# Attention and a residual MLP in one kernel: beta's rows on GpSimd, a later a1 and token mix, and the third batch's late q

## The chip, the cores and the metric

The kernel runs on one core of a Trainium2 chip. The time is the device time of one launch in microseconds (us), the median of several runs. A profile is one further execution, taken by the hardware profiler; its span is a little shorter than the device time. Five engines work side by side: TensorE (PE, matmuls; its weight loads are listed as PEld), VectorE (DVE), ScalarE (ACT), GpSimd (POOL) and SyncE (SP, which here only issues transfers). "L410" is line 410 of the kernel.

## The reference, cut to what matters

Eight batches of 384 tokens. Grouped attention (16 query heads, 4 key heads, head size 64) gives x of width 1024, and x goes through a residual MLP with a mix over tokens and one over channels:

```python
scores = scale * np.matmul(q, k.transpose(0, 1, 3, 2))
attn = np.exp(scores - max) / (sum + 1e-09)
x = np.matmul(attn, v)                       # (B, 384, 1024)

a1 = alpha1 * x + beta1
tok = np.einsum('ts,bsd->btd', w_tok, a1)    # mix over the 384 tokens
u = x + lam * tok
a2 = alpha2 * u + beta2
ch = np.maximum(a2 @ w_ch1, 0.0) @ w_ch2     # 1024 -> 4096 -> 1024
out = u + lam * ch
```

All inputs are float32 in DRAM; the kernel casts to bfloat16 while loading or afterwards.

## The kernel before

One batch's MLP is "main(b)": 32 tiles of h (w_ch1 times a2, ReLU), then six tiles of ch (w_ch2 times hT). The attention, token mix and transposes of batch b + 1 are "side(b + 1)", small pieces of work that are put between the matmuls of main(b) at numbered steps. w_ch1 is streamed again for each batch through a ring of five chunks; w_ch2 is loaded once, during the first batch. The first batch's own attention, side(0), has nothing to hide behind: it runs alone at the start.

Loads and transposes of k and q (k2 holds k twice, side by side; "flip" is a DMA transpose into kT or qT):

```python
def load_q(b):
    qrs[b] = sb.tile([P, Hq, NST, D], bf, tag="q_raw", name="q_raw", bufs=1)
    for h in range(0, Hq, G):
        nc.gpsimd.dma_start(out=qrs[b][:, h:h + G], in_=q[b, h:h + G]...)

def flip_queue(b):
    return nc.scalar if b == 2 else nc.sync

def flip_q(b, i=0, n=NP):
    flip_queue(b).dma_start_transpose(out=qT[:, i:i + n]..., in_=qrs[b][:, 2 * i:2 * (i + n)]...)
```

In the first batch (`first`), the normalization of one pair of heads, a1 and the token mix:

```python
def av_piece(p, hh):
    ...                                              # 18 matmuls for the pair p
    nc.vector.reciprocal(out=rinv, in_=av[:, :, :, D:])
    nc.vector.tensor_tensor(out=x[:, :, cols(p)]..., in0=av[...], in1=rinv..., op=MUL)
    if first:
        a1s[p] = hTf[...]                            # three places in turn
        nc.vector.tensor_tensor(out=a1s[p], in0=x[:, :, cols(p)], in1=bc(g1, p), op=MUL)
        return
    ...

def tok(p):
    ps = bank([P, NST, P], "mm", "tok") if first else ...
    for tt in range(NST):
        for st in range(NST):
            nc.tensor.matmul(out=ps[:, tt, :], lhsT=wtokT[...], rhs=a1s[p][:, st, :], ...)
        if first:
            nc.tensor.matmul(out=ps[:, tt, :], lhsT=R[...], rhs=H[:, cols(p)], ...)  # beta's part
    nc.vector.tensor_tensor(out=u, in0=ps, in1=u, op=ADD)
```

Scores go to PSUM banks "sc", of which there are two in side(0), and exp on ScalarE empties them. The order of side(0): 18 steps, each begins with scores(i), and behind it come the listed pieces. `ut` is the transpose of u (a2_transpose), `h_part` the first matmuls of main(0), `wtok_transpose` turns w_tok, `scale_rows` and `split` prepare alpha1 (row 0), beta1 (row 1) and alpha2, beta2 (rows 2, 3) in two bfloat16 parts, `spread` copies such a row to all partitions with a matmul, `rows_r` and `fill_h` build R and H for beta's part of the token mix:

```python
at = {0: [(warmup, 3), (scale_rows, 0), (split, 0, 1, 0)], 1: [(k_transpose, 1, 1), (split, 0, 1, 1)],
      2: [(q_transpose, 2, 2, "av")], 3: [(warmup, 1), (spread, lower, (0, 1), "tp")],
      4: [(av, 0)], 5: [(wtok_transpose, 0, "av"), (wtok_transpose, 1, "tp")],
      6: [(av, 1), (wtok_transpose, 2, "av"), (k_transpose, 2, 2, "tp")], 7: [(q_transpose, 4, 2, "av"), (scale_rows, 1), (split, 1, 2)],
      8: [(fill_h, 0), (rows_r, "tp"), (av, 2)], 9: [(spread, upper, (0, 1), "av", "ACT"), (q_transpose, 6, 2, "mm")],
      10: [(tok, 0)],
      11: [(av, 3)], 12: [(tok, 1), (ut, 0)], 13: [(av, 4), (tok, 2)], 14: [(ut, 1), (fill_h, 4), (tok, 3)],
      15: [(av, 5), (ut, 2)], 16: [(tok, 4), (ut, 3)], 17: [(av, 6), (tok, 5)]}
```

The weight ring in main(b), the load of the third batch (index 2), and where its flips stand in main(1) (steps 46 to 62 of the 64 half-tiles of h):

```python
            if b or c + RING < NCH:
                load_w1(b * NCH + c + RING)
            ...
            if b == 0 and c == NCH - 1:
                for i in range(RING):
                    load_w1(NCH + i)
                load_next(2)              # place_k twice, load_q, load_v
...
            if b == 1:
                moves = [(0, 46 + 4 * i, flip_q, 2, 2 * i - 2, 2) if i else (0, 46, flip_k, 2) for i in range(5)]
```

The issues of GpSimd at the start:

```python
load_v(0)
nc.gpsimd.dma_start(out=wtok_in, ...)
load_q4(2)
load_q4(3)
place_k(0, 0, (0,))
for c in range(RING):
    load_w1(c)
place_k(0, 1)            # casts k on GpSimd
```

Of the kernel before, what the change touches and what calls it, by code (L numbers as in the profile page):

```python
# [12 lines left out]
def kernel(  # L13
# [21 lines left out]
    nc = tc.nc  # L35
# [3 lines left out]
    RELU = mybir.ActivationFunctionType.Relu  # L39
    MUL = mybir.AluOpType.mult  # L40
    ADD = mybir.AluOpType.add

    B, Hq, S, D = q.shape
    Hkv = k.shape[1]
# [3 lines left out]
    P = 128  # L48
    NST = S // P
# [3 lines left out]
    NP = Hq // 2  # L53
# [3 lines left out]
    RING = 5  # L57
# [56 lines left out]
        for h in range(0, Hq, G):  # L114
            nc.gpsimd.dma_start(out=qrs[b][:, h:h + G], in_=q[b, h:h + G].rearrange("h (p st) d -> p h st d", st=NST))

    def flip_queue(b):
        return nc.scalar if b == 2 else nc.sync

    def flip_k(b):  # L120
        flip_queue(b).dma_start_transpose(out=kT.rearrange("p st h s -> p (st h) s"),
                                    in_=k2s[b].rearrange("p st h a d -> p (st h a d)"))

    def flip_q(b, i=0, n=NP):
        flip_queue(b).dma_start_transpose(out=qT[:, i:i + n].rearrange("p a j s -> p (a j) s"),
                                    in_=qrs[b][:, 2 * i:2 * (i + n)].rearrange("p h st d -> p (h st d)"))

    w1src = moe_w_ch1.rearrange("(dt di) nf -> di dt nf", di=P)
# [45 lines left out]
    def side(b):  # L174
# [8 lines left out]
        def cols(p):  # L183
            return slice(p * P, (p + 1) * P)
# [54 lines left out]
        def av_piece(p, hh):  # L239
            if hh == 0:  # L240
                if first:
                    avs[p] = bank([P, 2, NST, D1], "mm", "av")
                else:
                    avs[p] = three()[:, 0].rearrange("p k s -> p (k s)")[:, :2 * NST * D1].rearrange(
                        "p (h st d) -> p h st d", h=2, st=NST)
            av = avs[p]
            hk = (2 * p + hh) // G
            for sq in range(NST):
                m = NST * hh + sq
                for sk in range(NST):  # L250
                    k = (p * NST + sk) * NST + m // 2
                    nc.tensor.matmul(out=av[:, hh, sq, :], lhsT=ess[k // 4][:, m % 2, k % 4, :],  # L252
                                     rhs=vb[:, sk, hk, :], start=(sk == 0), stop=(sk == NST - 1))
            if hh == 0:
                return
            rinv = sb.tile([P, 2, NST, 1], f32, tag="rinv", name="rinv", bufs=1)
            nc.vector.reciprocal(out=rinv, in_=av[:, :, :, D:])  # L257
            nc.vector.tensor_tensor(out=x[:, :, cols(p)].rearrange("p st (h d) -> p h st d", h=2), in0=av[:, :, :, :D],  # L258
                                    in1=rinv.to_broadcast([P, 2, NST, D]), op=MUL)
            if first:  # L260
                a1s[p] = hTf[:, 6144 + p % 3 * S:6144 + (p % 3 + 1) * S].rearrange("p (a d) -> p a d", a=NST)
                nc.vector.tensor_tensor(out=a1s[p], in0=x[:, :, cols(p)], in1=bc(g1, p), op=MUL)
                return
            t = sb.tile([P, NST, P], f32, tag="tmp", name="a1f", bufs=4)
            nc.vector.tensor_tensor(out=t, in0=x[:, :, cols(p)], in1=bc(g1, p), op=MUL)  # L265
            a1s[p] = sb.tile([P, NST, P], bf, tag="a1", name="a1", bufs=2)
            nc.vector.tensor_tensor(out=a1s[p], in0=t, in1=bc(h1, p), op=ADD)  # L267

        def tok(p):
            ps = bank([P, NST, P], "mm", "tok") if first else three()[:, 0, :NST]  # L270
# [79 lines left out]
        if not first:  # L350

            turns = {}
            if b == 1:
# [19 lines left out]
        ut = a2_transpose  # L373
        at = {0: [(warmup, 3), (scale_rows, 0), (split, 0, 1, 0)], 1: [(k_transpose, 1, 1), (split, 0, 1, 1)],
              2: [(q_transpose, 2, 2, "av")], 3: [(warmup, 1), (spread, lower, (0, 1), "tp")],
              4: [(av, 0)], 5: [(wtok_transpose, 0, "av"), (wtok_transpose, 1, "tp")],
              6: [(av, 1), (wtok_transpose, 2, "av"), (k_transpose, 2, 2, "tp")], 7: [(q_transpose, 4, 2, "av"), (scale_rows, 1), (split, 1, 2)],
              8: [(fill_h, 0), (rows_r, "tp"), (av, 2)], 9: [(spread, upper, (0, 1), "av", "ACT"), (q_transpose, 6, 2, "mm")],
              10: [(tok, 0)],
              11: [(av, 3)], 12: [(tok, 1), (ut, 0)], 13: [(av, 4), (tok, 2)], 14: [(ut, 1), (fill_h, 4), (tok, 3)],  # L380
              15: [(av, 5), (ut, 2)], 16: [(tok, 4), (ut, 3)], 17: [(av, 6), (tok, 5)]}
        for i in range(18):
            add(scores, i)
            for f, *a in at.get(i, []):
                add(f, *a)
        for f, *a in ((ut, 4), (h_part, (0, 1), range(4)), (av, 7), (ut, 5), (tok, 6),
                      (h_part, (2, 3), range(4)), (h_part, range(4), (4,)), (ut, 6), (tok, 7),
                      (h_part, range(4), (5,)), (ut, 7), (h_part, range(4), (6,)), (h_part, range(4), (7,))):
            add(f, *a)
        return us  # L390
# [8 lines left out]
    def main(b):  # L399
# [3 lines left out]
        for c in range(NCH):  # L403
            w1 = w1_tiles.pop(b * NCH + c)
            for j in range(CW):
                nt = c * CW + j
                begun = b == 0 and nt in early
                ps = early[nt] if begun else bank([P, 512], "mm", "h")
                for dt in range(0 if begun else NDT):
                    nc.tensor.matmul(out=ps[:, :n], lhsT=w1[:, dt, j * P:(j + 1) * P],  # L410
                                     rhs=a2T[:, dt, :n], start=(dt == 0), stop=(dt == NDT - 1))
                    if dt == 3:
                        yield 0
                c1 = bias1[:, nt:nt + 1]
                if b == 0:
                    evac("DVE" if nt % 2 else "ACT")(out=c1, in_=ps[:, S:n])
                if nt % 2 == 0:
                    nc.scalar.activation(out=hT[:, nt, :], in_=ps[:, :S], func=RELU, bias=c1)  # L418
                else:
                    nc.vector.tensor_scalar(out=hT[:, nt, :], in0=ps[:, :S], scalar1=c1,  # L420
                                            scalar2=0.0, op0=ADD, op1=mybir.AluOpType.max)
                yield 0

            if b or c + RING < NCH:
                load_w1(b * NCH + c + RING)
            if b == 0 and c == NCH - RING:
                for i in range(3, 8):
                    load_w2(0, i, 8)
                for i in range(8):
                    load_w2(1, i, 8)  # L430
            if b == 0 and c == NCH - 1:
                for i in range(RING):
                    load_w1(NCH + i)
                load_next(2)
        for dw in range(NDW):
            cs = slice(dw * 512, (dw + 1) * 512)
            for ms in range(NST):
# [17 lines left out]
    with tc.manual_schedule(engines=order):  # L455
# [59 lines left out]
                nc.vector.tensor_reduce(out=t[:n], in_=ident[:n, :n].rearrange("p (k c) -> p c k", c=NP), op=ADD, axis=AX)  # L515


        def scale_rows(i):
            r = rows_f[:, i * P:(i + 1) * P]
            nc.vector.tensor_tensor(out=r, in0=r, in1=rows_f[:, 3 * P:4 * P], op=MUL)  # L520


        def split(lo, hi, step=None):
            c = slice(lo * P, hi * P)
            for i, m in enumerate(masks[:2]):
                if step in (None, i):
                    src, dst = (rows_t, rows_f) if i else (rows_f, rows_t)
                    nc.vector.tensor_copy(out=rows_b[:32, c], in_=src[:, c])
                    nc.vector.scalar_tensor_tensor(out=dst[:, c], in0=rows_b[:32, c], scalar=m, in1=src[:, c],
                                                   op0=MUL, op1=mybir.AluOpType.subtract)  # L530
            if step != 0:
                nc.vector.tensor_copy(out=rows_b[:32, c], in_=rows_f[:, c])


        def fill_h(p):
# [2 lines left out]
                                    in1=sel4[:, p:p + 4, None].to_broadcast([32, 4, P]), op=MUL)  # L538

        load_v(0)  # L540
        nc.gpsimd.dma_start(out=wtok_in, in_=moe_w_tok.rearrange("(p tt) s -> p tt s", tt=NST))
        load_q4(2)
        load_q4(3)
        place_k(0, 0, (0,))
        for c in range(RING):
            load_w1(c)
        place_k(0, 1)

        load_k(1)
        load_q(1)  # L550
# [8 lines left out]
        for b in range(B):  # L559
            us = side(b + 1) if b + 1 < B else ({}, {})  # L560


            moves = []
            if b == 1:
                moves = [(0, 46 + 4 * i, flip_q, 2, 2 * i - 2, 2) if i else (0, 46, flip_k, 2) for i in range(5)]
            if 0 < b < B - 2:
                moves += [(1, 1, load_k, b + 2), (1, 2, load_next, b + 2), (1, 34, flip_k, b + 2), (1, 36, flip_q, b + 2, 0, 2),
                          (1, 37, flip_q, b + 2, 2, 2), (1, 42, flip_q, b + 2, 4, 2), (1, 43, flip_q, b + 2, 6, 2)]
            for i, u, *m in moves:
                us[i].setdefault(u, []).append(m)  # L570
            done = [0, 0]
            for second in main(b):
                if b == second - done[1] - 1 == 0:
                    lead_banks.close()
                    threes.append(ST(tc.psum_pool(name="threes", bufs=3)))
                for f, *a in us[second].get(done[second], []):
                    f(*a)
                done[second] += 1
# [28 lines left out]
```

The softmax here doesn't subtract the row's maximum and nothing guards it: scores larger than these inputs give would overflow.

## Time and profile before

| | |
|---|---|
| time, median of 3 runs | 806.16 us (805.33 to 807.13) |
| span of the profiled run | 803.5 us, granted TensorE clock 1.000 |
| TensorE busy | 793.8 us, 6123 matmuls |
| w_ch chunks loaded | 144 of 512 KB (as written), issued by GpSimd, median 8.6 us to landing |
| DMA traffic | 113.17 MB, mean 141 GB/s |
| first batch's side(0) | ends at 38.48 us, when main(0)'s own h begins |
| second batch's h | begins at 133.44 us |
| third batch's h | begins at 232.67 us |

An entry of the timeline gives the start, the duration, the engine, the line, the operation, the tiles, how many instructions were merged, and in brackets how long the engine had stood idle before and who released it. Matmul ends are modelled, so small holes between matmuls can be hidden in a "busy" TensorE; differences of starts are safer than durations.

### The profile page before, as it was taken

The page shows a single profiled execution, that of the slowest core. Times are in us where ns is not written, and L with a number is a line of the kernel's source. Part 1 is how long each engine was busy: PE and PEld are TensorE (multiplying, and loading weights), DVE is VectorE, ACT ScalarE, POOL GpSimd, SP SyncE. Part 2 cuts the span into 40 slices and gives each one's busy share as a digit, 9 for nine tenths or more (in the row PEclk, how much of TensorE's full clock was granted, in tenths as well). Part 3 has the DMA queues.
Part 4 walks back from the last instruction along what each step waited for, and adds up shares of the span by engine and source line. Part 5 has one row for each costly group of instructions (what it writes and reads, how often), then busy time and mean ns, then how long its engine had stood idle before and what let it go on. Part 6 is the DMA issues. An engine that isn't in the chain of part 4 may idle for free.

```text
span 803.5 us, 14220 instructions
## 1 busy us (share of the span) xinstructions
PE 793.8 (99%) x6123; PEld 452.0 (56%) x6123; DVE 343.5 (43%) x669; ACT 226.9 (28%) x309; POOL 178.5 (22%) x233
## 2 busy tenths in 40 slices
PE   8999999999999999999999999999999999999997
PEld 4766555655556555565555655566555655556545
DVE  8652465215552266322662236622366225552122
ACT  6624431223402233123221233122431223312100
POOL 7234231332013500135002340033400330003000
PEclk9999999999999999999999999999999999999999
DMA  9999999999269972999439991499914995129611
GB/s 190 202 186 202 205 207 170 187 186 170 66 126 188 198 101 58 162 189 196 74 73 169 193 196 43 92 174 197 163 46 114 165 198 88 48 61 187 82 40 40
DMA packets 234975, 113.17 MB, mean 141 GB/s; under 512 B 84376, under 2 KB 228768, under 8 KB 234912
## 3 DMA queue, kind: packets, MB, share of 16 engines
q0 software_dynamic: 170752, 83.47, 79.1%
q1 hardware_dynamic: 58848, 27.22, 13.5%
q10 hardware_dynamic: 5312, 1.57, 1.5%
q8 instruction: 48, 0.79, 0.4%
q14 instruction: 15, 0.12, 0.0%
HBM read 170.53 MB, written 12.58 MB: 228 GB/s over the span
## 4 chain that ended last, share of the span: by engine, by line
PE 84%; DMA 10%; issue 3%; DVE 1%; POOL 1%; ACT 0%; POOLq 0%
PE ch L443 37%; PE h L410 34%; DMA w<-in_moe_w_ch_dram 8%; PE sc L217 4%; PE sc L252 3%; PE sc L273 3%; DMA qT<-q_raw 1%; POOL w L136 1%; PE h L168 1%; PE tok L273 1%; PE av L252 0%; PE warm L460 0%; PE ut L290 0%; PE tp L203 0%; ACT hT L226 0%
## 5 line engine op out<-in xcount | busy, mean ns | idle before, releaser
L443 PE MATMUL ch<-w,hT 128*128 128x512 bf16 (+2 forms) x1600 | 357.7, 371 | 1.1 <-DVE o L448 0.9
L410 PE MATMUL h<-a2T,w 128*128 128x384 bf16 (+1 forms) x2016 | 331.5, 326 | 0.8 <-ACT hT L418 0.8
L410 PEld LDWEIGHTS <-w 128*128 128x128 bf16 x2016 | 196.8, 98 | 131.2 <-issue 1.5
L443 PEld LDWEIGHTS <-hT 128*128 128x128 bf16 x1600 | 144.6, 98 | 153.1 <-issue 10.5
L136 POOL DMA_DIRECT2D w<-in_moe_w_ch_dram x128 | 112.1, 878 | 519.3 <-PE h L410 500.5
L226 ACT ACTIVATE es<-sc 128x1024 bf16<-128x1024 f32 x126 | 121.4, 1023 | 187.9 <-PE sc L217 175.8
L420 DVE TENSOR_SCALAR hT<-h,bias 128x384 bf16<-128x384 f32 x128 | 79.1, 618 | 218.3 <-PE h L410 217.7
L418 ACT ACTIVATE hT<-h,bias 128x384 bf16<-128x384 f32 x128 | 74.3, 580 | 304.9 <-PE h L410 299.4
L448 DVE TENSOR_TENSOR o<-ch,vecs 128x512 f32<-128x512 f32 (+2 forms) x50 | 33.4, 669 | 107.8 <-PE ch L443 107.8
L252 PEld LDWEIGHTS <-es 128*128 128x128 bf16 x1008 | 38.2, 97 | 13.2
L273 PEld LDWEIGHTS <-wtokT 128*128 128x128 bf16 x576 | 37.3, 98 | 13.8 <-DVE x L258 1.7
L217 PE MATMUL sc<-qT,kT 64*128 64x384 bf16 (+2 forms) x576 | 41.9, 272 | 0.7 <-DMA qT<-q_raw 0.6
L257 DVE RECIPROCAL rinv<-sc 128x6 f32<-128x6 f32 x56 | 10.8, 193 | 68.4 <-PE sc L252 67.5
L252 PE MATMUL sc<-v,es 128*128 128x65 bf16 x1008 | 39.9, 193 | 0.0
L280 DVE TENSOR_TENSOR x<-sc,x 128x384 f32<-128x384 f32 x56 | 31.0, 553 | 20.0 <-PE sc L273 20.0
L273 PE MATMUL sc<-a,wtokT 128*128 128x128 bf16 x504 | 37.3, 219 | 0.0
L217 PEld LDWEIGHTS <-kT 64*128 64x128 bf16 x576 | 21.6, 94 | 24.5 <-issue 18.2
L449 DVE TENSOR_TENSOR o<-o,x 128x512 f32<-128x512 f32 (+2 forms) x50 | 33.5, 670 | 1.7
L284 DVE TENSOR_TENSOR a<-x,vecs 128x384 bf16<-128x384 f32 x56 | 32.7, 584 | 1.9
L265 DVE TENSOR_TENSOR a1f<-x,vecs 128x384 f32<-128x384 f32 x56 | 31.2, 558 | 1.9
L267 DVE TENSOR_TENSOR a<-a1f,vecs 128x384 bf16<-128x384 f32 x56 | 31.2, 558 | 1.9
L258 DVE TENSOR_TENSOR x<-sc,rinv 128x384 f32<-128x384 f32 x56 | 31.2, 558 | 1.9
(75 smaller groups left out, 203.1 us busy)
## 6 DMA issues: line engine op xcount, KB each, us to landing
w<-in_moe_w_ch_dram POOLq DMA_DIRECT2D x144, 512.0 KB, 8.6
out_dram<-o SPq DMA_DIRECT2D x47, 256.0 KB, 2.0
q_raw<-in_q_dram POOLq DMA_DIRECT2D x28, 192.0 KB, 8.1
kst<-in_k_dram SPq DMA_DIRECT2D x16, 192.0 KB, 3.4
v<-in_v_dram POOLq DMA_DIRECT2D x24, 64.0 KB, 7.9
a2T<-a SPq DMA_TRANSPOSE x56, 2.3
qg<-in_q_dram POOLq DMA_DIRECT2D x3, 192.0 KB, 5.9
stage<-in_q_dram ACTq DMA_DIRECT2D x2, 192.0 KB, 3.7
```

Source lines behind the costliest of these rows:

```text
L136: nc.gpsimd.dma_start(out=t, in_=w1src[:, :, c * CW * P:(c + 1) * CW * P])
L217: nc.tensor.matmul(out=sc[:, hh, k % 4:k % 4 + n], lhsT=kT[r, sk, 2 * p // G, :], rhs=qT[r, p, st:st + n, :], start=True, stop=True)
L226: nc.scalar.activation(out=e, in_=sc, func=EXP, scale=scale_qk)
L252: nc.tensor.matmul(out=av[:, hh, sq, :], lhsT=ess[k // 4][:, m % 2, k % 4, :], rhs=vb[:, sk, hk, :], start=(sk == 0), stop=(sk == NST - 1))
L273: nc.tensor.matmul(out=ps[:, tt, :], lhsT=wtokT[:, st, tt * P:(tt + 1) * P], rhs=a1s[p][:, st, :], start=(st == 0), stop=(st == NST - 1 an ...
L284: nc.vector.tensor_tensor(out=a2s[p], in0=u, in1=bc(al2, p), op=MUL)
L410: nc.tensor.matmul(out=ps[:, :n], lhsT=w1[:, dt, j * P:(j + 1) * P], rhs=a2T[:, dt, :n], start=(dt == 0), stop=(dt == NDT - 1))
L418: nc.scalar.activation(out=hT[:, nt, :], in_=ps[:, :S], func=RELU, bias=c1)
L420: nc.vector.tensor_scalar(out=hT[:, nt, :], in0=ps[:, :S], scalar1=c1, scalar2=0.0, op0=ADD, op1=mybir.AluOpType.max)
L443: nc.tensor.matmul(out=ps[:, lo:hi], lhsT=hT[:, nt, ms * P:(ms + 1) * P], rhs=w2[:, nt, dw * 512 + lo:dw * 512 + hi], start=(nt == 0), sto ...
L448: nc.vector.tensor_tensor(out=o[:, lo:hi], in0=ps[:, lo:hi], in1=lam_t[:, c], op=MUL)
L449: nc.vector.tensor_tensor(out=o[:, lo:hi], in0=o[:, lo:hi], in1=x[:, ms, c], op=ADD)
```

## The change

For the third batch: q is loaded later, behind the last w_ch1 chunk of the second batch, so that it does not stand in the stream before; the flips of k and q go to SP's queue; k is turned at the second batch's first step, q in four parts as they land. For the first batch: beta1's row is scaled and split on GpSimd, early; k's cast on GpSimd comes before most weight chunks; q's third group is loaded before w_tok; w_tok's transposes come later; a1 is a piece of its own, apart from AV; the token mix begins three steps later; the upper half of alpha1's spread is emptied by VectorE and not by ScalarE.

```diff
-    def flip_queue(b):
-        return nc.scalar if b == 2 else nc.sync
     def flip_q(b, i=0, n=NP):
-        flip_queue(b).dma_start_transpose(...)
+        nc.sync.dma_start_transpose(...)            # flip_k likewise
...
             if first:
-                a1s[p] = hTf[...]
-                nc.vector.tensor_tensor(out=a1s[p], in0=x[:, :, cols(p)], in1=bc(g1, p), op=MUL)
                 return
+        def a1(p):
+            a1s[p] = hTf[...]
+            nc.vector.tensor_tensor(out=a1s[p], in0=x[:, :, cols(p)], in1=bc(g1, p), op=MUL)
...
-              4: [(av, 0)], 5: [(wtok_transpose, 0, "av"), (wtok_transpose, 1, "tp")],
-              6: [(av, 1), (wtok_transpose, 2, "av"), (k_transpose, 2, 2, "tp")], 7: [(q_transpose, 4, 2, "av"), (scale_rows, 1), (split, 1, 2)],
-              8: [(fill_h, 0), (rows_r, "tp"), (av, 2)], 9: [(spread, upper, (0, 1), "av", "ACT"), (q_transpose, 6, 2, "mm")],
-              10: [(tok, 0)],
-              11: [(av, 3)], 12: [(tok, 1), (ut, 0)], 13: [(av, 4), (tok, 2)], 14: [(ut, 1), (fill_h, 4), (tok, 3)],
-              15: [(av, 5), (ut, 2)], 16: [(tok, 4), (ut, 3)], 17: [(av, 6), (tok, 5)]}
+              4: [(av, 0)], 5: [(a1, 0)], 6: [(av, 1), (k_transpose, 2, 2, "tp")],
+              7: [(q_transpose, 4, 2, "av"), (a1, 1)], 8: [(av, 2)],
+              9: [(wtok_transpose, 0, "av"), (wtok_transpose, 1, "tp")],
+              10: [(wtok_transpose, 2, "av"), (q_transpose, 6, 2, "mm"), (fill_h, 0)], 11: [(av, 3), (rows_r, "tp")],
+              12: [(spread, upper, (0, 1), "av"), (a1, 2)], 13: [(tok, 0), (av, 4), (a1, 3)],
+              14: [(tok, 1), (ut, 0), (a1, 4)], 15: [(av, 5), (tok, 2), (a1, 5), (fill_h, 4)], 16: [(ut, 1), (tok, 3)],
+              17: [(ut, 2), (av, 6), (a1, 6)]}
...
-        for f, *a in ((ut, 4), (h_part, (0, 1), range(4)), (av, 7), (ut, 5), (tok, 6),
-                      (h_part, (2, 3), range(4)), (h_part, range(4), (4,)), (ut, 6), (tok, 7),
+        for f, *a in ((tok, 4), (ut, 3), (h_part, (0, 1), range(3)), (av, 7), (a1, 7), (tok, 5), (ut, 4), (h_part, (0, 1), (3,)),
+                      (tok, 6), (h_part, (2, 3), range(4)), (ut, 5), (tok, 7), (h_part, range(4), (4,)), (ut, 6),
                       (h_part, range(4), (5,)), (ut, 7), (h_part, range(4), (6,)), (h_part, range(4), (7,))):
...
             if b == 0 and c == NCH - 1:
                 for i in range(RING):
                     load_w1(NCH + i)
-                load_next(2)
+                place_k(2, 0)
+                place_k(2, 1)
+                load_v(2)
+            if b == 1 and c == NCH - RING - 1:
+                load_q(2)
...
+        def split(lo, hi, step=None, eng=nc.vector):
+            ...                                   # on GpSimd: tensor_scalar, then tensor_tensor,
+            ...                                   # for VectorE's one scalar_tensor_tensor
...
         load_v(0)
+        load_q4(2)
         nc.gpsimd.dma_start(out=wtok_in, ...)
-        load_q4(2)
         load_q4(3)
         place_k(0, 0, (0,))
-        for c in range(RING):
+        load_w1(0)
+        load_w1(1)
+        place_k(0, 1)
+        scale_rows(1, nc.gpsimd)
+        split(1, 2, None, nc.gpsimd)
+        for c in range(2, RING):
             load_w1(c)
-        place_k(0, 1)
...
             if b == 1:
-                moves = [(0, 46 + 4 * i, flip_q, 2, 2 * i - 2, 2) if i else (0, 46, flip_k, 2) for i in range(5)]
+                moves = [(0, 1, flip_k, 2)] + [(0, 46, flip_q, 2, i, 2) for i in range(0, NP, 2)]
```

More of the change, by code (lines that the diff above doesn't have):

```diff
@@ L41 @@
     ADD = mybir.AluOpType.add
+    SUB = mybir.AluOpType.subtract
     B, Hq, S, D = q.shape
@@ L115, in load_q @@
             nc.gpsimd.dma_start(out=qrs[b][:, h:h + G], in_=q[b, h:h + G].rearrange("h (p st) d -> p h st d", st=NST))
-    def flip_queue(b):
-        return nc.scalar if b == 2 else nc.sync
     def flip_k(b):
-        flip_queue(b).dma_start_transpose(out=kT.rearrange("p st h s -> p (st h) s"),
+        nc.sync.dma_start_transpose(out=kT.rearrange("p st h s -> p (st h) s"),
                                     in_=k2s[b].rearrange("p st h a d -> p (st h a d)"))
     def flip_q(b, i=0, n=NP):
-        flip_queue(b).dma_start_transpose(out=qT[:, i:i + n].rearrange("p a j s -> p (a j) s"),
+        nc.sync.dma_start_transpose(out=qT[:, i:i + n].rearrange("p a j s -> p (a j) s"),
                                     in_=qrs[b][:, 2 * i:2 * (i + n)].rearrange("p h st d -> p (h st d)"))
@@ L260, in av_piece @@
             if first:
-                a1s[p] = hTf[:, 6144 + p % 3 * S:6144 + (p % 3 + 1) * S].rearrange("p (a d) -> p a d", a=NST)
-                nc.vector.tensor_tensor(out=a1s[p], in0=x[:, :, cols(p)], in1=bc(g1, p), op=MUL)
                 return
@@ L267, in av_piece @@
             nc.vector.tensor_tensor(out=a1s[p], in0=t, in1=bc(h1, p), op=ADD)
+        def a1(p):
+            a1s[p] = hTf[:, 6144 + p % 3 * S:6144 + (p % 3 + 1) * S].rearrange("p (a d) -> p a d", a=NST)
+            nc.vector.tensor_tensor(out=a1s[p], in0=x[:, :, cols(p)], in1=bc(g1, p), op=MUL)
         def tok(p):
@@ L515, with scale_rows @@
                 nc.vector.tensor_reduce(out=t[:n], in_=ident[:n, :n].rearrange("p (k c) -> p c k", c=NP), op=ADD, axis=AX)
-        def scale_rows(i):
+        def scale_rows(i, eng=nc.vector):
             r = rows_f[:, i * P:(i + 1) * P]
-            nc.vector.tensor_tensor(out=r, in0=r, in1=rows_f[:, 3 * P:4 * P], op=MUL)
-        def split(lo, hi, step=None):
+            eng.tensor_tensor(out=r, in0=r, in1=rows_f[:, 3 * P:4 * P], op=MUL)
+        def split(lo, hi, step=None, eng=nc.vector):
             c = slice(lo * P, hi * P)
@@ L527, in split @@
                     src, dst = (rows_t, rows_f) if i else (rows_f, rows_t)
-                    nc.vector.tensor_copy(out=rows_b[:32, c], in_=src[:, c])
-                    nc.vector.scalar_tensor_tensor(out=dst[:, c], in0=rows_b[:32, c], scalar=m, in1=src[:, c],
-                                                   op0=MUL, op1=mybir.AluOpType.subtract)
+                    eng.tensor_copy(out=rows_b[:32, c], in_=src[:, c])
+                    if eng is nc.vector:
+                        eng.scalar_tensor_tensor(out=dst[:, c], in0=rows_b[:32, c], scalar=m, in1=src[:, c],
+                                                 op0=MUL, op1=SUB)
+                    else:
+                        eng.tensor_scalar(out=dst[:, c], in0=rows_b[:32, c], scalar1=m, scalar2=None, op0=MUL)
+                        eng.tensor_tensor(out=dst[:, c], in0=dst[:, c], in1=src[:, c], op=SUB)
             if step != 0:
-                nc.vector.tensor_copy(out=rows_b[:32, c], in_=rows_f[:, c])
+                eng.tensor_copy(out=rows_b[:32, c], in_=rows_f[:, c])
         def fill_h(p):
```

## The prediction

> **What bounds the kernel now.** The page's first part comes first: who is busy.
>
> ```profile
> PE 793.8 (99%) x6123; PEld 452.0 (56%) x6123; DVE 343.5 (43%) x669; ACT 226.9 (28%) x309; POOL 178.5 (22%) x233
> ```
>
> TensorE is idle for 803.5 - 793.8 = 9.7 us of the span. The change adds and removes no matmul: the instruction order has the same number of TensorE rows before and after. So it can only win idle time of TensorE, and the next question is where the 9.7 us lie. The chain that ended last, in order of time, shows the same picture in every batch from the third on: 41.60 us of h, then the ch stretch, without a foreign step between.
>
> ```profile
> 232.67 41.60 PE h L410 x256
> ...
> 329.31 41.60 PE h L410 x256
> ...
> 715.90 41.60 PE h L410 x256
> 757.50 38.04 PE ch L443 x192
> ```
>
> 329.31 - 232.67 = 96.64 us is a batch at full TensorE rate; nothing in the diff touches it. What can move lies before 232.67. There I split the span by windows: columns are the stretch, then busy time of PE, weight loads, DVE, ACT and POOL, clock, DMA share, GB/s.
>
> ```profile
> 4.66:9.33 4.67, 4.47 (x42) 2.32 (x43) 3.61 (x11) 3.70 (x6) 4.67 (x7) 1.00 1.53 193
> 9.33:20.06 10.73, 8.64 (x136) 5.66 (x134) 9.81 (x27) 8.37 (x10) 6.32 (x10) 1.00 1.43 207
> 20.06:29.95 9.89, 9.89 (x174) 7.84 (x172) 7.61 (x17) 8.86 (x11) 3.81 (x6) 1.00 1.51 194
> 29.95:38.48 8.53, 8.52 (x86) 6.00 (x84) 4.35 (x10) 2.85 (x6) 0.53 (x1) 1.00 1.42 199
> ```
>
> In the first batch's attention TensorE loses 10.73 - 8.64 = 2.09 us between 9.33 and 20.06, where VectorE is busy 9.81 of 10.73 us. The waits of TensorE in that stretch give the three holes:
>
> ```profile
> PE tok L273 <- DVE x L258: 1.4, 1, 1.4
> PE tp L203 <- DVE wtokT L305: 0.4, 1, 0.4
> PE tp L192 <- POOL k L106: 0.2, 1, 0.2
> ```
>
> The second place is the second batch's main part, in the TensorE timeline:
>
> ```profile
> 167.60 2.76 PE L410 MATMUL h<-a2T,w 128*128 128x384 bf16 x16 [0.19 <-ACT hT L418]
> 170.59 2.76 PE L410 MATMUL h<-a2T,w 128*128 128x384 bf16 x16 [0.23 <-ACT hT L418]
> 173.77 2.76 PE L410 MATMUL h<-a2T,w 128*128 128x384 bf16 x16 [0.41 <-ACT hT L418]
> 176.75 1.02 PE L443 MATMUL ch<-w,hT 128*128 128x512 bf16 x4 [0.23 <-ACT hT L418]
> 178.42 0.83 PE L217 MATMUL sc<-qT,kT 64*128 64x384 bf16 x12 [0.64 <-DMA qT<-q_raw]
> ```
>
> Its h starts at 133.44. An undisturbed batch has its first ch 41.60 us later (175.04) and its first scores another 0.86 us later (175.90). Here they come at 176.75 and 178.42: 178.42 - 175.90 = 2.52 us late, of which 1.71 us stand before ch and 0.81 us before the scores. The ScalarE timeline says why: each of the five DMA transposes issued from ACT's queue holds it about 3 us, between the hT evictions that TensorE waits for.
>
> ```profile
> 163.78 3.14 ACTq L121 DMA_TRANSPOSE kT<-k  x1
> 166.97 0.58 ACT L418 ACTIVATE hT<-h,bias 128x384 bf16<-128x384 f32 x1 [2.85 <-PE h L410]
> 166.99 2.92 ACTq L125 DMA_TRANSPOSE qT<-q_raw  x1
> ```
>
> **What the Trainium skill says.** "DMA: Bandwidth & Descriptors", section "Issuing engines are not separate DMA queues": transfers of SP, ACT and GpSimd run on the same 16 DMA engines and interleave, and another issuer saves only sequencer time. The trace agrees on sharing: the transpose of k lands after 11.3 us beside the weight loads and after 4.5 us (median) in the later batches, where the weight ring is full. It shows that issuing is not small, though: 2.9 to 3.7 us on ACT against 1.24 us for the same q transpose on SP. The section "Queues, rings and completion order" of that page says that each DMA engine takes turns between the queues that have work, so a transpose need not wait behind the whole weight backlog. Its agreement: k landed at 163.78 + 11.3 = 175.1 and the first q transpose at 166.99 + 11.29 = 178.28, 3.2 us behind it. "GPSIMD Engine Reference", section "4.1 Engine selection", puts two-input elementwise work on GpSimd at about twice VectorE's time. No run here shows that yet; GpSimd only casts in this trace (128x384, 0.53 us).
>
> **The change, part by part.**
>
> *(a) First batch: VectorE relieved and reordered.* Out of VectorE go scale_rows(1) and split(1,2), six small instructions from 14.94 to 16.82 in its timeline: 0.27 + 0.21 + 0.34 + 0.34 + 0.34 + 0.21 = 1.7 us busy, 1.9 us with gaps. In comes the eviction of the upper spread, which ACT did in 0.58 us and VectorE does in 0.69 us (its row for the lower spread). Net 1.2 us less in front of the first token mix. AV now comes earlier and the weight transposes later, and a1 (0.56 us each) no longer stands between AV's normalization and the next copy. The k copy on GpSimd, now behind two weight issues instead of five (0.9 us each), ends near 10.2 instead of 12.6, so the hole of 0.2 us closes.
> I walk the new order forward with durations of the rows (scores 0.33, AV 0.6, tok 0.70, a 2-pair transpose 0.43, exp 0.93 back to back). With two score banks scores(6) needs exp 4, which ends at about 11.1, while TensorE is ready at 10.64 as the weight transposes no longer fill that place: a new hole of 0.4. The third weight transpose waits for the copy of the first: 0.4. Token mix 1 waits for token mix 0's addition on VectorE: 0.3 to 0.4. At the tail the last u transpose no longer stands right behind its token mix (0.16 won). Old holes 2.09 + 0.16 = 2.25; new ones 1.2. Gain: 1.0 us.
>
> *(b) The same gain at the DMA.* Weight chunk 5 lands at 38.61 + 7.0 = 45.6, and TensorE begins it near 46.6: 1.0 us of slack. Then w2's eighth slice lands at 68.7 + 16.9 = 85.6 and is used at 86.70: 1.1 us. Traffic is near 200 GB/s all the time to 38, so those landings move with TensorE only in part. A gain of 1.0 us just fits; one of 2 would be partly handed back. That is why I don't put (a) higher.
>
> *(c) GpSimd's new work.* Eight small instructions at perhaps 0.4 to 0.6 us (VectorE's 0.21 to 0.34, about doubled) make 3 to 5 us between w1 issues 1 and 2. Issue 2 moves from 8.8 to about 14. The weights already queued land until 19.5 (8.03 + 11.5), so the DMA engines do not run dry. Cost: 0. Beta's row is wanted by fill_h near 17, after it is done.
>
> *(d) Second batch: transposes on SP.* The five issues leave ACT, so the four hT waits and the delay of ch go: 1.71 us. k is transposed at once behind the last output of the first batch, near 135, far ahead. q's load now follows the second batch's last weight chunk: with h starting at T, that chunk is issued at T + 29.1 (162.50 in the trace), q's first part at T + 30.0. Chunks land 7.9 us after issue there, so the chunk lands near T + 37.0 and q's 192 KB, at 197 GB/s 1.0 us, near T + 38.0. SP then needs 1.24 us to issue and, beside the weights, the 3.2 us measured above: T + 42.4 to 42.8 with hand-overs. The scores want it at T + 41.60 + 0.86 = T + 42.46. Wait left: about 0.3 us. Gain: 2.52 - 0.3 = 2.2, say 2.1 us, as semaphore hand-overs are not all counted.
>
> Sum: 1.0 + 2.1 = 3.1 us; 806.16 - 3.1 = 803.1 us. All else (d) touches, k and q of the fourth batch, has tens of us of room.
>
> **The rivals.** First: the late q simply replaces the removed wait. For it: q's load starts 60 us later than before (163.4 instead of 103.80), and a transpose beside weights has taken 11.3 us. If the first q transpose took 7 to 8 us, scores would start at T + 45.5, and (d) would give nothing or lose 0.5; the time would be 805 to 806. Against it: the 11.3 us include a queue of its own kind (k, twice the size, with a 3.14 us issue). Second: VectorE stays the bound of the first batch, or exp does, and (a) gives nothing: 804. For it: VectorE is at 91% there, and ACT at 78%. Third: (a) frees the full 2.2 us and DMA keeps up: 801.9. Against it stands the slack of 1.0 us in (b). Fourth: GpSimd's work delays the weight stream, and TensorE waits for chunk 2 or later: 1 to 3 us lost, 805. Against it: chunk 2 landed at about 22 and is first used at 38.48.
>
> **Range and chances.** (a) lies between 0 and 2 us, (d) between 0 and 2.5; the measured runs of before spread by 1.8 us. 801.8 to 805.2 us should hold 8 times in 10. Two per cent are 16 us, more than all of TensorE's idle time, so faster by 2% is all but excluded, and slower would need a stall that nothing here shows.
>
> **What would show it.** (a): the 1.4 us wait of tok for VectorE is gone, small ones appear at scores, a weight transpose and the second tok, and the first main h begins 1 us earlier than 38.48. (d): no wait of h for hT in the second batch, h to ch in 41.6 us, scores after T + 42.5 with a wait for qT under 1 us; the third batch's h starts near 229.6 instead of 232.67. Wrong if qT's wait is 2 us or more, if h of the first batch waits for w, or if batches after the third are not 96.6 us.

## The result and the profile after

| | before | changed |
|---|---|---|
| time, median | 806.17 us (805.33 to 807.13, 4 runs) | 808.27 us (807.98 to 809.6, 4 runs) |
| ratio to before | | 1.0029, 95% interval 1.0012 to 1.0046 |
| span of the profiled run | 803.5 us | 806.2 us |
| first batch's side(0) ends (first own h of main) | 38.48 us | 36.78 us |
| second batch's h begins (T) | 133.44 us | 132.03 us |
| third batch's h begins, after T | 99.06 us | 103.19 us |

The change is slower, by 2.1 us where 3.1 us of gain were predicted. The last two rows split it: 1.41 us are won up to T and 4.13 us are lost in the second batch. (They are read from the TensorE timeline, which has the third batch's h at 232.50 and 235.22 us; the chain of waits has both 0.16 us later.) From the third batch's h on nothing moves. The chain in order of time (start, duration, work) has 332.02 - 235.38 = 96.64 us from h to h, as before:

```profile
235.38 41.60 PE h L411 x256
332.02 41.60 PE h L411 x256
```

**First batch.** Windows of the changed kernel (columns as in the prediction), and what TensorE waited for between 4 and 37 us:

```profile
9.58:20.50 10.92, 10.40 (x179) 7.05 (x179) 9.54 (x24) 10.62 (x12) 9.70 (x17) 1.00 1.39 207
```

```profile
PE sc L215 <- ACT hT L224: 0.5, 1, 0.5
PE sc L215 <- ACT qT L203: 0.2, 1, 0.2
```

The 2.09 us of idle TensorE in this stretch have become 0.52. TensorE no longer waits for VectorE. ScalarE, with its exponentials, now stands at 10.62 of 10.92 us, and the largest wait left, the 0.5 us of the scores, is for it; that it is the next bound is likely and was not tested.

**Second batch.** The chain of waits there:

```profile
161.97 9.46 DMA q_raw<-in_q_dram
...
171.44 7.92 DMA qT<-q_raw
...
180.88 4.64 PE ch L448 x16
```

The scores in TensorE's timeline, and the ch stretch behind the scores in the chain of the kernel before:

```profile
179.50 1.38 PE L215 MATMUL sc<-qT,kT 64*128 64x384 bf16 x12 [4.84 <-DMA qT<-q_raw]
```

```profile
179.25 3.56 PE ch L443 x16
```

q's first part takes 9.46 us to land and its transpose 7.92 us. The scores begin at T + 47.47, 5.0 us behind the undisturbed T + 42.46 (before: 2.52 us behind). There is a second loss: 16 ch matmuls take 4.64 us here and 3.56 us at the same place of the kernel before, 12 score matmuls 1.38 us instead of 0.83, together 1.6 us. The windows say why; the third figure from the right is the granted clock:

```profile
173.63:179.50 5.87, 0.98 (x6) 0.33 (x5) 0.62 (x1) 0.00 (x0) 0.87 (x1) 1.00 1.39 188
179.50:183.00 3.50, 3.50 (x18) 1.59 (x19) 0.00 (x0) 2.85 (x3) 0.00 (x0) 0.52 1.36 184
183.00:185.00 2.00, 2.00 (x11) 0.93 (x10) 0.00 (x0) 0.00 (x0) 0.00 (x0) 0.99 1.34 183
```

After a hole of 4.84 us TensorE works at about half clock for 3.5 us, which costs 3.5 x (1 - 0.52) = 1.7 us by this reckoning, close to the 1.6 us of the two lines. 5.0 + 1.6 us explain the second batch, which is 103.19 - 96.64 = 6.55 us too long.

### The profile page after: what moved, and what is told of

The parts are those of the page before. It is cut to its first block, busy times and chain, and to the rows that moved or that the text cites. A ratio compares the mean times of both kernels' runs of the same rounds, so it can differ in the third digit from the quotient of the medians.

```text
span 806.2 us, 14156 instructions
## 1 busy us (share of the span) xinstructions
PE 789.8 (98%) x6056; PEld 453.5 (56%) x6123; DVE 341.4 (42%) x664; ACT 226.4 (28%) x308; POOL 182.5 (23%) x241
## 4 chain that ended last, share of the span: by engine, by line
PE 92%; DMA 5%; issue 2%; POOL 1%; DVE 0%; ACT 0%; POOLq 0%
PE ch L448 41%; PE h L411 38%; PE sc L215 4%; PE sc L250 4%; PE sc L273 4%; DMA q_raw<-in_q_dram 3%; DMA w<-in_moe_w_ch_dram 1%; DMA qT<-q_raw 1%; POOL w L134 0%; PE warm L465 0%; PE tp L201 0%; ACT hT L224 0%; PE vec L330 0%; POOL w L139 0%; POOL hT L538 0%
## 5 line engine op out<-in xcount | busy, mean ns | idle before, releaser
L448 PE MATMUL ch<-w,hT 128*128 128x512 bf16 (+2 forms) x1533 | 347.1, 371 | 4.4 <-issue 1.1
L215 PE MATMUL sc<-qT,kT 64*128 64x384 bf16 (+2 forms) x576 | 42.4, 274 | 6.6 <-DMA qT<-q_raw 4.8
```

What stands on the lines that cost most here:

```text
L215: nc.tensor.matmul(out=sc[:, hh, k % 4:k % 4 + n], lhsT=kT[r, sk, 2 * p // G, :], rhs=qT[r, p, st:st + n, :], start=True, stop=True)
L448: nc.tensor.matmul(out=ps[:, lo:hi], lhsT=hT[:, nt, ms * P:(ms + 1) * P], rhs=w2[:, nt, dw * 512 + lo:dw * 512 + hi], start=(nt == 0), sto ...
```

## The experiments

"Before" was run beside each; ratios are to it, with 95% intervals. T and the length from T to the third batch's h come from the profiles.

### The two halves apart

First batch only: the changed kernel with the third batch's loads and flips as before.

```diff
-        nc.sync.dma_start_transpose(...)            # flip_k, flip_q
+        flip_queue(b).dma_start_transpose(...)      # ACT for b == 2
...
+                load_q(2)                           # at the end of the first batch's h
...
-            if b == 1 and c == NCH - RING - 1:
-                load_q(2)
...                                                  # moves of b == 1 as before
```

> The first batch's change alone; loads, flips and queues of the third batch as before. Theory: 1.7 us earlier at the end of side(0), 0.26 us given back at weight chunk 5: 806.2 - 1.4 = 804.8 us, third batch's h at about 231.2. Rival: the slack of the weight stream hands the gain back before the third batch: 806.

Measured: 803.71 us, ratio 0.9968 (0.9955 to 0.998). side(0) ends at 36.45, T is 131.50, length 98.86 us. The first batch's part is a gain, and larger than thought (2.9 us against 1.4).

The late q only: the kernel before with the change's load_q(2) and its flips on SP.

> The late q and the flips on SP alone; first batch as before. Theory: scores 5.0 us late instead of 2.52, then 1.6 us lost at half clock: 806.2 + 2.5 + 1.6 = 810.3 us, wait for qT 4.8 us, granted clock about 0.5 for 3 us behind it. Rival: the wait comes from the first batch's earlier end (less time for DMA); then wait for qT under 4 us and about 808 us.

Measured: 810.03 us, ratio 1.0046 (1.0033 to 1.0058); wait for qT 5.0 us, T 133.55, length 103.88 us. From its chain:

```profile
173.41 7.95 DMA qT<-q_raw
```

The wait is there without the earlier end of the first batch, so the rival falls: the new handling of q alone makes the loss. The two halves, 2.9 us won and 3.5 us lost, add up to 0.6 us lost, while the changed kernel's runs gave 2.1; the three intervals reach 1.0 to 1.4 us to each side, so both can stand, and the size of each half is known to about 1 us.

### The clock

```diff
-                0: [(scores3, 0)], 4: [(av, 0)], ...
+                0: ([(warmup, 27)] if b == 2 else []) + [(scores3, 0)], 4: [(av, 0)], ...
```

> The changed kernel with 27 matmuls of 128x384 (4.4 us, their result is not used) in front of the third batch's first scores, in the place of the wait for qT. Theory: the idle TensorE loses its clock, which costs 1.6 us after the wait; the filler keeps it, the wait itself stays: 808.3 - 1.6 = 806.7 us, clock 1.000. Rival: the half clock has another cause, or costs nothing: 808.3 us or more.

Measured: 806.58 us, ratio 1.0001 (0.9992 to 1.0009): 1.7 us better than the changed kernel, with 27 matmuls more. From T to the third batch's h its profile has 101.47 us, 1.72 less than the changed kernel's 103.19. Its TensorE timeline:

```profile
175.14 4.55 PE L465 MATMUL warm<-wtokT 128*128 128x384 bf16 x27
180.04 0.83 PE L215 MATMUL sc<-qT,kT 64*128 64x384 bf16 x12 [0.35 <-DMA qT<-q_raw]
180.80 3.63 PE L448 MATMUL ch<-w,hT 128*128 128x512 bf16 x15
```

The scores come no earlier (T + 47.38), but they and the ch behind them run at full rate (0.83 and 3.63 us). So the clock's share of the loss is shown.

### Where q may stand in the stream

q loaded where it was before, its transposes on SP (only the load is moved back):

> The changed kernel, but the third batch's q is loaded where it was before (at the end of the first batch's h), and still turned on SP as it lands. Theory: the loss lies in the late q alone (5.0 us late in the second batch against 2.52 before, and 1.6 us of half clock behind it), the first batch's change is a gain of 1.4 us. Then no wait for qT and no ACT hold-up is left: 806.2 - 1.4 - 2.5 = 802.2 us, clock 1.000, third batch's h at about 228.9. Rival (why the author moved it): q and four transposes in the weight stream make the second batch's first weight chunks late; then h of the second batch waits for w and the time is 804 or more.

Measured: 808.4 us, ratio 1.0024 (1.0017 to 1.0032). The theory fell, the rival holds. That the transposes stand at step 46 of the program does not hold SP back: they go out right behind k's, in the first third of h. SP's queue, then the first and largest hole of TensorE:

```profile
135.99 9.63 SPq L123 DMA_TRANSPOSE qT<-q_raw  x4
```

```profile
150.27 2.77 PE L411 MATMUL h<-a2T,w 128*128 128x384 bf16 x16 [2.16 <-DMA w<-in_moe_w_ch_dram]
```

With 1.52, 0.61 and 0.49 us further on, h waits 4.8 us for weights. TensorE eats a 512 KB chunk in 2.60 us of h, which is about 200 GB/s, and that is what the DMA engines move in all in that phase (198 and 197 GB/s in the changed kernel's windows from 158 to 163 and from 163 to 168 us): extra traffic there delays the chunks.

The late load 3 chunks earlier (7.8 us), and 1 chunk earlier (2.6 us):

```diff
-            if b == 1 and c == NCH - RING - 1:
+            if b == 1 and c == NCH - RING - 4:      # one chunk: NCH - RING - 2
```

> The changed kernel with q's load three chunks (7.8 us) earlier in the weight stream of the second batch. Theory: q and its transposes fit while five chunks are ahead; no wait for qT is left, and h waits for weights little (under 1.5 us, as 3.9 us of q stand in front of chunks that have about 5 us of slack): 803.7 - 2.5 = 801.5 to 803 us. Rival, from the run with q before the stream: any q traffic and transposes ahead of the last chunks cost h 4 to 5 us; then 808.

Measured: 809.08 us, ratio 1.0034 (1.0022 to 1.0047).

> The changed kernel with q's load one chunk (2.6 us) earlier. Theory: the wait for qT falls from 4.8 to about 2.2 us, and a hole that short leaves the clock alone (before had 0.64 us and full clock): 808.3 - 2.6 - 1.6 = 804.1 us. Rival: a 2.2 us hole also halves the clock: 805.7 us.

Measured: 807.78 us, ratio 1.0017 (1.0008 to 1.0026). In both the wait for qT is gone and h waits instead; the line of each (3 chunks, then 1):

```profile
169.48 8.15 PE L411 MATMUL h<-a2T,w 128*128 128x384 bf16 x32 [3.74 <-DMA w<-in_moe_w_ch_dram]
```

```profile
175.18 2.77 PE L411 MATMUL h<-a2T,w 128*128 128x384 bf16 x16 [3.36 <-DMA w<-in_moe_w_ch_dram]
```

Neither forecast for one chunk holds. For three chunks the wait is 4.1 us in all, and half clock behind it adds to it: the first ch begins at T + 48.79 instead of T + 41.60. So q's load inside this stretch of the weight stream, or its transposes early in it, make h wait 3 to 5 us, and a load behind the last chunk comes too late for the scores. What is left is the load in front of the stream, as the kernel before had it, with the transposes held back.

### Why the transpose took 7.9 us

The five chunks behind q were placed later in the program:

> The changed kernel, but the five weight chunks of the third batch that follow q in the stream are held back until the second batch's h is done. Theory: the first q transpose takes 7.9 us because the weight stream shares the DMA engines; beside q's own three parts alone it takes 3 to 5 us, the wait for qT falls from 4.8 to 1 to 2 us, TensorE keeps its clock: 808.3 - 3.3 - 1.6 = 803.4 us. Rival: the transpose is slow by itself or by q's other parts (192 KB each); then it stays at 7 to 8 us and the time at 808.

Measured: 808.61 us, ratio 1.0028 (1.0016 to 1.0039). This decided nothing: GpSimd issued the chunks at the old times (165.59, 166.98, ... us), as each issue waits only for the h that frees its place in the ring, wherever its line stands in the program. Held by a dependency instead:

```diff
+            if b == 1 and c >= NCH - RING:
+                if c == NCH - 1:
+                    nc.gpsimd.dma_start(out=gate[:1], in_=hT[:1, 30, :2])   # waits for the 31st tile of h
+                    for i in range(RING):
+                        load_w1(2 * NCH + i)
```

> The changed kernel, with the five weight chunks behind q truly held: GpSimd, which ran ahead in the earlier attempt and issued them at the same times as before, now first waits for the 31st tile of h (a 4-byte transfer). Theory: the q transpose takes 7.9 us because it shares the DMA engines with weights (three times as many weight packets as its own in that stretch); alone beside q's parts it takes 3 to 5 us, wait for qT 0 to 2 us: 808.3 - 3.5 - 1.6 = 803.2 us. Rival: four transposes issued together slow each other; then 7 to 8 us again, 808.5.

Measured: 802.37 us, ratio 0.9953 (0.9939 to 0.9967), length 97.75 us. The chain of this kernel:

```profile
162.21 9.56 DMA q_raw<-in_q_dram
171.79 4.01 DMA qT<-q_raw
```

q lands as before, its transpose in half the time; the scores wait 1.03 us. What the queues did during the first transpose (packets, MB, share of 16 engines; q0 holds GpSimd's loads, q1 SP's transfers), in the changed kernel from 171.5 to 179:

```profile
q0 software_dynamic: 2607, 1.21, 122.2%
q1 hardware_dynamic: 849, 0.21, 21.6%
```

and with the chunks held, from 171.5 to 175:

```profile
q0 software_dynamic: 759, 0.28, 67.6%
q1 hardware_dynamic: 812, 0.20, 62.7%
```

About the same number of transpose packets, 3.1 packets of GpSimd's loads beside each in the first and 0.9 in the second (the rest of q). The turns between the queues, on which the prediction counted, came to three packets of loads for one of the transpose. The rival, four transposes that slow each other, falls.

### Versions that keep both

q loaded early; q's transposes on SP held by a 4-byte transfer that waits for the 23rd tile of h; k turned on SP in the first batch's ch stretch:

```diff
+            if b == 0:
+                moves = [(1, 36, flip_k, 2)]
             if b == 1:
-                moves = [(0, 1, flip_k, 2)] + [(0, 46, flip_q, 2, i, 2) for i in range(0, NP, 2)]
+                moves = [(0, 46, hold, 22)] + [(0, 46, flip_q, 2, i, 2) for i in range(0, NP, 2)]
+    def hold(nt):
+        nc.sync.dma_start(out=gate[:1], in_=hT[:1, nt, :2])
```

> q loaded early as before; k turned on SP in the first batch's ch stretch; q's four transposes on SP, held back by a 4-byte transfer on SP that waits for the 23rd tile of h, so that they start behind the issue of the second batch's last weight chunk. Theory: neither the weight stream (h waited 4.8 us where the transposes ran early) nor the scores suffer, ScalarE is free: 803.7 - 2.5 = 801.3 us, no wait of h or scores above 0.3 us. Rival: the transposes at that place still delay the last two chunks: h waits 1 us or more, 802.5 or above.

Measured: 804.95 us (803.64 to 807.6), ratio 0.9985 (0.9973 to 0.9997). The twelve runs fall into two groups: six with a granted clock of 1.000 took 803.64 to 804.39 us, six with 0.996 to 0.998 took 805.52 to 807.60. In the profile, that of a run of 807.17 us, neither h nor scores wait for q or weights, but h begins late, and half clock follows:

```profile
135.74 43.82 PE L415 MATMUL h<-a2T,w 128*128 128x384 bf16 x250 [2.90 <-DMA a2T<-a]
```

```profile
135.74:140.00 4.26, 4.18 (x13) 1.82 (x13) 0.62 (x1) 0.58 (x1) 0.37 (x1) 0.50 0.09 34
```

k's transpose stood on SP in front of the last two a2 transposes, which h needs. With k's behind them (step 42 in place of 36):

> As the gated kernel, but k is turned behind the last transposes of the second batch's a2, not in between, where it made them late (h waited 2.9 us for a2T and lost clock behind it). q's transposes are held until the 23rd tile of h. Theory: nothing waits; against the first batch's change alone the 2.5 us of the second batch are gone: 803.7 - 2.4 = 801.3 us. Rival: the stream has no room at either place; h or scores wait 1.5 us or more, 803 us.

Measured: 801.38 us (801.01 to 803.12), ratio 0.9946 (0.9933 to 0.9958): better than both kernels. TensorE behind the last h, T being 131.64:

```profile
173.24 1.03 PE L451 MATMUL ch<-w,hT 128*128 128x512 bf16 x4
174.20 0.83 PE L219 MATMUL sc<-qT,kT 64*128 64x384 bf16 x12
```

Scores at T + 42.56, no wait in brackets, and 96.65 us to the third batch's h (228.29): the second batch is now as long as any other.

The same, with k and q both turned in the idle stretch in front of the second batch's h, unheld:

> q loaded early; k and q turned on SP directly behind the last a2 transposes, in the stretch before the second batch's h where the DMA engines stood idle (share 0.19 for 4 us). Theory: five of the ten us of transposing fit in the idle stretch; the rest delays weights, which have some 4 us of slack: h waits 0 to 1 us, 801.5 us. Rival: transposes in early h cost their full time as before: h waits 2 to 3 us, with clock loss 804 to 806.

Measured: 804.22 us, ratio 0.9974 (0.9964 to 0.9984); h waits 0.86 and 0.91 us for weights, length 99.13 us. It lies between the two; probably part of the transposing still falls into h.

### The first batch's two parts

Both start from kernels named above. The new order alone (beta's split back on VectorE, step 7):

> The first batch's change alone, but beta's row scaled and split on VectorE at step 7 as before. Theory: VectorE was the bound (9.81 of 10.73 us busy), its 1.9 us come back into the path before the third group's q copy: side(0) ends 1 to 1.9 us later than with GpSimd, 803.7 + 1.5 = 805.2 us. Rival: the new order alone wins, VectorE has slack in it: 803.7 to 804.

Measured: 806.48 us, ratio 1.0007 (0.9998 to 1.0015).

GpSimd's part with its order of loads (beta's row, k's cast and q's third group sooner), in the old order of side(0):

> The kernel before, with nothing changed but GpSimd's part at the start: beta's row scaled and split there, k's cast and q's third group sooner. Order of AV, a1, weight transposes and token mix as before. Theory: VectorE's relief is most of the gain of the first batch (with the new order alone, the time was that of before): side(0) ends 1.0 to 1.9 us earlier than 38.48, 806.4 - 1.5 = 804.9 us. Rival: relief and order only work together, as token mix 0 is still wanted too early; then the end of side(0) stays within 0.5 us of 38.48 and the time at 806.

Measured: 805.67 us, ratio 0.9989 (0.998 to 0.9997). TensorE's largest hole with the new order alone, and the one that the old order keeps with the split on GpSimd:

```profile
18.12 0.33 PE L305 MATMUL tp<-ident,stage 128*128 128x128 bf16 x3 [1.97 <-DVE wtokT L308]
```

```profile
15.42 0.49 PE L204 MATMUL tp<-ident,qg 128*128 128x128 bf16 x6 [0.74 <-DVE wtokT L306]
```

In the new order VectorE's six instructions (15.11 to 16.8 us) stand in front of the weight transposes' copies, and the token mix's hole comes back under another name. Alone, order gives nothing and relief 0.9 us; together they give 2.9 us in the timed runs of the first experiment. side(0) ends at 39.21 with the order alone, later than the theory's 36.45 + 1.9, and at 38.76 with GpSimd's part alone, within 0.5 us of 38.48 as its rival said: order and relief work mostly together. How much of the 2.9 us is due to that is not sure. Both profiles also lost 0.24 and 0.71 us of TensorE beside k's early cast, as the last section shows, which the first experiment's profile did not, and how often this happens in the timed runs is not known.

## Why the prediction was wrong, by its steps

- *The bound and the places of idle time:* right. Only the first batch and the second batch's end moved; every later batch kept 96.6 us.
- *(a), 1.0 us:* right in kind, on the small side in size. The changed kernel's side(0) ends 1.70 us earlier; with the old handling of q it was 2.03, close to the third rival. Over all eleven profiles of this first batch it is 0.77 to 2.25 us. The hole of the scores came as drawn (0.46 us against 0.4), the other new ones were smaller: scores to third weight transpose 0.1 instead of 0.4, second token mix 0.2 instead of 0.3 to 0.4. The last section says what makes the start shift from one profile to another.
- *(b), slack of the weight stream:* right for the changed kernel. Chunk 5's weight load waited 0.47 us for its DMA in the changed kernel, and chunk to chunk TensorE lost about 0.3 us: 1.70 won at side(0) are 1.41 at T. It is no fixed price: in the version that took 801.38 us, 1.80 us won at side(0) are still 1.80 at T, and with the first batch's part alone 2.03 are 1.94.
- *(c), GpSimd's eight instructions:* right. They ran from 9.77 to 14.0 us (the two-input scaling took 0.52 us against 0.27 on VectorE, near the doubling assumed), the third chunk was issued at 13.96 (predicted "about 14"), and no h waited for it.
- *(d), ScalarE freed:* right, 1.71 us of hT waits are gone. *(d), q in time:* this step failed. q was issued at T + 29.9 as predicted. It landed at T + 39.4 and not T + 38.0, as the chunk in front of it takes 9.3 us from issue to landing and not 7.9. This was misread in the trace of before: the chunk issued at 162.50 took 9.4 us there, and 7.9 us are those of the two chunks ahead of it. The transpose was put at 1.24 + 3.2 us and measured 7.92. The 3.2 us are the distance between two landings of transposes that were under way together; that is not the time of one. The run with the weights held gives the size of the term left out, 7.92 - 4.01 = 3.9 us for sharing the engines with weights. Of the 4.9 us between the predicted T + 42.4 and the measured T + 47.3, 1.4 are q's landing and 3.5 the transpose.
- *The rival that was put aside:* "if the first q transpose took 7 to 8 us" was what happened, and it was thought to cost nothing or 0.5 us. The scores came 5.0 us late, as q also landed late, and a term was in neither sum: half clock behind the hole, 1.7 us by the filler.
- *Together:* expected for the second batch 2.1 us less, measured 4.13 more, a difference of 6.2. About 4.7 us of it are the wait (5.0 instead of 0.3) and 1.6 us the clock.

What stays open: which length of a hole costs the clock. Of the profiles here holes of 2.90, 3.74 and 4.84 us were followed by about half clock, one of 3.36 us was not (granted clock 1.00 from 175.18 to 179 us), nor were those of 2.16 us and less. As 2.90 us cost it and 3.36 us did not, the length alone does not decide. The profile with 3.36 us is that of 805.89 us, the only one of its kernel's twelve runs with a granted clock of 1.000; the other eleven had 0.996 to 0.998 and took 806.97 to 809.39 us. The kernel with 2.90 us kept 1.000 in half of its runs. How long the hole was in the runs without a profile is not known. The Trainium skill's "TensorE: Matmul & The Clock Gate", section "What's actually happening", says that activity is judged in free-running windows of about 3.4 us. That fits holes of like length ending differently. But the 2.90 us that were enough are less than a whole such window, and no run here was made to settle it.

## What to carry to other kernels

A transfer that frees the stream at one place must be asked what it will share the engines with at its new place; the landing time of such a transfer is measured there and not taken from a quiet stretch or from two overlapping ones. In a kernel whose weight stream runs at the rate of the DMA engines, put loads into the phase with slack, and hold transposes back by a true dependency until the last needed weight is on its way: moving the line in the program does not delay an engine whose issue waits for nothing else. A hole of some us in TensorE can cost clock on top (1.7 us behind 4.84 here); independent matmuls in the hole keep it.

## What the hardware showed that was not expected

- Small VectorE instructions at the start do not always take the same time. In the profile of GpSimd's part alone, a two-input VectorE instruction took 1.02 us beside GpSimd's cast of k, and TensorE waited 0.71 us behind it. VectorE, then GpSimd in that profile, then the same VectorE instruction in the changed kernel's:

```profile
8.99 1.02 DVE L531 SCALAR_TENSOR_TENSOR hT<-hT,stage 32x128 f32<-32x128 bf16 x1
```

```profile
8.84 1.03 POOL L107 CAST k<-kst 128x384 bf16<-128x384 f32 x2
```

```profile
8.37 0.34 DVE L535 SCALAR_TENSOR_TENSOR hT<-hT,stage 32x128 f32<-32x128 bf16 x1
```

In the changed kernel it started before that cast (8.85) and took 0.34 us. The Trainium skill's "SBUF — State Buffer", section "Who interferes with whom", says that a VectorE instruction with two SBUF inputs contends with a GpSimd instruction that reads SBUF, and that the order of issue decides which of the two is blocked; 8.99 lies just behind 8.84, which agrees. So do the other profiles with the early cast: where the instruction starts at 8.12 to 8.39 us (five profiles) it takes 0.34 us, where it starts at 8.98 to 9.00 (eight) it takes 0.58 or 1.02. With the same first batch, side(0) ends at 36.23 to 36.78 in the former and at 37.31 to 37.71 in the latter. So bringing k's cast forward puts it beside the split of alpha's row, and which of the two comes first moves the end of the first batch by 0.5 to 1.5 us. This was seen in profiles and not tested by a run of its own.
- A transpose of 192 KB beside the weight stream took 7.9 us, with 3.1 packets of the other queue for each of its own, and 4.0 us without the weights.
